# Blocks 4 and 5 of a convolution feeding a gated feed-forward block: from time-major matmuls to channel-major taps

## The chip, the cores and the metric

The kernel runs on one core of one Trainium2 chip. The time is device microseconds (us) of one launch; the kernel before takes 771.22 us, the median of three runs between 770.91 and 771.37 us. Times inside the launch are counted from the start of the profile's span.

The core's engines work through instruction queues of their own, each in the order in which the program gave them: PE (matmuls), ACT, DVE and POOL (element-wise work), and SP, which here only issues transfers. POOL also issues transfers: those that change the type on the way (float32 to float16) are all issued from it.

## The reference

`x` has 8 sequences of 4096 rows (time) with 192 columns (channels). First a causal convolution over time with 7 taps, one softmax-normalised set of taps for each of 8 heads of 24 channels; then a feed-forward block on the 32768 rows:

```python
out[b, s, h, :] = sum(w[h, k] * x_pad[b, s + k, h, :] for k in range(7))
g = y @ w_gate                      # y: (32768, 192), w_gate: (192, 1536)
silu = g * (1.0 / (1.0 + np.exp(-g)))
return (silu * (y @ w_val)) @ w_out # (32768, 192), float32
```

## The kernel before

**Blocks and steps.** The rows are cut into 64 blocks of 512. The inner width of 1536 is cut into 12 chunks of 128, so the work is 768 steps (`n`), 12 for a block; within a block a step is `j`, 0 to 11. Step `n` runs `gate_val` (L734): twelve half-height matmuls of 512 columns in pairs (gate and val side by side) for one chunk, in three pairs over the three channel tiles of the block; ACT then applies Silu (L752) and DVE multiplies by val (L754). At every step with `j` of 1, 4, 7 or 10 a `slot` (L802) runs 24 matmuls of the product with `w_out`; so PE's pattern is three steps and one slot. The slot at `j` of 4 ends a block: ACT and DVE copy the result out of PSUM and SP issues the store.

**The block's input.** `gate_val` needs the convolved block with channels on partitions, as three tiles of float16, `xc[b][0..2]`. They are made in two ways.

- *Time-major, by PE:* blocks 0 to 5. For blocks 2 to 5 `early_pair` (L379) makes two blocks at once: rows are loaded by POOL in windows (tile `xp`), doubled by SP (`twice`), multiplied with a banded matrix of the taps in 64 matmuls of 120 columns (L394), and copied out by ACT and DVE (L411, L422). Blocks 3, 4 and 5 then go to DRAM (`eout`, L424, four transfers each) and come back transposed (`efetch`, L434, three DMA transposes each). `early_pair(2)` stands at step 19, `early_pair(4)` at step 27.
- *Channel-major, by ACT, DVE and POOL:* blocks 6 to 63, in units of four blocks (unit 1 holds blocks 4 to 7, unit 2 blocks 8 to 11). `cast_x` (L542, POOL's queue) copies a unit of `x` to DRAM as float16; `turn_x` (L560, SP's queue) fetches it transposed, two DMA transposes a block; `join_x` (L569) puts the third 64 channels of two blocks side by side. Then three *jobs* for each two blocks (`conv_job`, L580): the first 128 channels of the even block, the shared 64 channels of both ("pair"), and the first 128 channels of the odd block. A job has seven taps: tap 0 on ACT into `total`, taps 1 and 2 on DVE into `total` (L618), taps 3 and 4 on ACT into tiles of their own (L643), which POOL adds (L593), and taps 5 and 6 on POOL, a product (L608) and an addition each. `place` (L653) then copies the shared channels and the joined ones to where `gate_val` reads them: four transfers on SP.

**What sets the order.** The order on each engine is written out by the program (`seq`, L71). `pooled_work` (L708), called once a step, hands out the taps: one DVE tap at `j` of 1, 7 and 10; one ACT tap at those and at 4, two at 10 of even blocks; so one job takes eight steps on average. POOL's part of a job is issued where the last tap before it is issued. A block is placed 14 steps after its last job was issued (`done + 14`), and not before 16 steps ahead of its first step. `planned` (L678) says for each unit at which step the cast, the transposes and the jobs are queued: the first cast at step 11, the next at 12, unit 3's at 56. On SP all transfers stand in one line: stores, transposes, joins and copies; a transfer that has to wait holds up all that stand behind it.

Of the kernel before, what the change touches and what calls it, by code (L numbers as in the profile page):

```python
# [10 lines left out]
def kernel(  # L11
# [422 lines left out]
    def efetch(b):  # L434
        xc[b] = []
        for k in range(SL):
            t = cpool.tile([P, XW], fp16, tag=f"xc{k}", name=f"xc{k}", bufs=8)
            seq(
                nc.sync.dma_start_transpose(
                    out=t[:, 0:TB], in_=scre[b][0:TB, Q * k : Q * k + P]  # L440
                )
            )
            xc[b].append(t)

    def eturn(b, where, then=None):
        c, j = (2, EO) if b < 2 else (4, CO)
        tiles = [
            cpool.tile([P, XW], fp16, tag=f"xc{k}", name=f"xc{k}", bufs=8)
            for k in range(SL)
        ]  # L450
# [28 lines left out]
        xc[b] = tiles  # L479
        if b == 0:  # L480
            copy_channel_taps()
# [41 lines left out]
        for m, name in enumerate(pick):  # L523
            taps[name] = both_taps[:, m * K : m * K + K]

    def first_of(u):
        return HALF if u == 1 else 0

    def head_x(u):
        rows = XP + UT - first_of(u) * TB  # L530
        xs[u] = dpool.tile([rows, D], fp16, tag="xs", name="xs")
        if u % upb == 0:
            seq(
                nc.sync.dma_start(
                    out=xs[u].rearrange("t d -> (t d)")[0 : XP * D].rearrange(
                        "(a n) -> a n", n=P
                    ),
                    in_=fill[0 : XP * D // P, :],
                )
            )  # L540

    def cast_x(u):  # L542
        t0 = u * UT + first_of(u) * TB
        rows = XP + u * UT + UT - t0
        flat = xs[u].rearrange("t d -> (t d)")
        skip = XP if u % upb == 0 else 0
        n = (rows - skip) * D // P
        seq(
            nc.gpsimd.dma_start(  # L549
                out=flat[skip * D : rows * D].rearrange("(a n) -> a n", n=n),  # L550
                in_=bass.AP(
                    tensor=x_flat.tensor,
                    offset=(t0 - XP + skip) * D,
                    ap=[[n, P], [1, n]],
                ),
                max_dma_last_dim=2048,
            )
        )

    def turn_x(u, i, at):  # L560
        r0 = TB * (i - first_of(u))
        rows = xs[u][r0 : r0 + TB + XP]
# [3 lines left out]
        seq(nc.sync.dma_start_transpose(out=t, in_=rows[:, at : at + P]))  # L566
        tiles[u, i] = t
# [1 line left out]
    def join_x(u, i):  # L569
        seq(nc.sync.dma_start(out=x12[u, 2 * i + 1][0:Q], in_=x12[u, 2 * i][Q:P]))  # L570

    FIRST, ON_DVE = 0, (1, 2)
# [7 lines left out]
    def conv_job(u, what, i):  # L580
        index = n_jobs[0]
        n_jobs[0] += 1
        on_act, on_pool = SHARES[index % len(SHARES)]
        job = {"dve": len(ON_DVE), "act": len(on_act), "parts": []}
        at = XP - pad

        def shifted(k):
            return job["src"][:, at + k : at + k + TB]

        def add(part, k):  # L590
            total = job["total"]
            seq(
                nc.gpsimd.tensor_tensor(  # L593
                    job["dst"] if k == K - 1 else total, total, part, op=ALU.add
                )
            )

        def proceed():
            if job["dve"]:
                return  # L600
            while job["parts"]:
                add(*job["parts"].pop(0))
            if job["act"]:
                return
            for k in on_pool:
                part = cpool.tile([P, TB], fp32, tag="piece", name="piece", bufs=2)
                seq(
                    nc.gpsimd.tensor_scalar(  # L608
                        part, shifted(k), scalar1=job["tap"][:, k : k + 1],
                        scalar2=1.0, op0=ALU.mult, op1=ALU.mult,  # L610
                    )
                )
                add(part, k)
            finished[u, what, i] = step_now[0]

        def dve_step(k):
            seq(
# [8 lines left out]
        def act_step(k):  # L626
# [10 lines left out]
                )  # L637
                dve_steps.extend((index, lambda k=k: dve_step(k)) for k in ON_DVE)
            else:
                part = cpool.tile([P, TB], fp32, tag="part", name="part", bufs=8)  # L640
                job["parts"].append((part, k))
# [9 lines left out]
        act_steps.extend((index, lambda k=k: act_step(k)) for k in (FIRST, *on_act))  # L651

    def place(u, i):  # L653
        b = UB * u + i
# [14 lines left out]
    plan = {}  # L669
    placing = []  # L670

    def queue_jobs(u):
        for i in range(first_of(u), UB, 2):
            for job in (("block", i), ("pair", i // 2), ("block", i + 1)):
                conv_job(u, *job)
        placing.extend((u, i) for i in range(first_of(u), UB))

    def planned(v):  # L678
        s0 = ustep * v
        turns = [  # L680
            turn
            for i in range(first_of(v), UB, 2)
            for turn in ((i, 0), (i, Q), (i + 1, Q), (i + 1, 0), (i // 2, None))
        ]
        if v == 1:
            head, cast, jobs = 10, 11, 27
            times = (20, 20, 20, 23, 23)
        elif v == 2:
            head, cast, jobs = 10, 12, 40
            times = (32, 33, 34, 35, 37, 38, 39, 40, 41, 43)  # L690
        elif v == 3:
            head, cast, jobs = 56, 56, 56
            times = range(66, 86, 2)
        else:
            head = cast = s0 - (115 if v > 4 else 100)
            jobs = s0 - 89
            first = s0 - (95 if v > 4 else 87)
            times = range(first, first + 20, 2)
        plan.setdefault(head, []).append(lambda: head_x(v))
        plan.setdefault(cast, []).append(lambda: cast_x(v))  # L700
# [5 lines left out]
        plan.setdefault(jobs, []).append(lambda: queue_jobs(v))  # L706

    def pooled_work(n, j):  # L708
        step_now[0] = n
        if j != 4:  # L710
            ready = dve_steps[0][0] if dve_steps else None
            if j in (1, 7, 10) and ready is not None:
                dve_steps.pop(0)[1]()
            for _ in range(2 if j == 10 and n // NCH % 2 == 0 else 1):
                ahead = act_steps[0][0] if act_steps else n_jobs[0]
                if j in (1, 7, 10) and act_steps and (
                    ready is None or ahead < ready + 3
# [2 lines left out]
        while placing:  # L720
# [133 lines left out]
    for v in range(1, NU):  # L854
        planned(v)

    for n in range(n_steps):
        b, j = divmod(n, NCH)
# [8 lines left out]
        elif j % 3 == 1 and n > 18:  # L867
# [63 lines left out]
```

## Time and profile before

| | before |
|---|---|
| median of 3 runs | 771.22 us |
| profiled execution, its own time | 771.32 us |
| its span in the profile | 769.5 us |
| TensorE clock granted | 1.00 |
| PE busy | 763.0 us, 99% of the span |
| DVE busy | 702.5 us, 91% |
| ACT busy | 649.1 us, 84% |
| POOL busy | 637.8 us, 83% |

The profiled execution's own time is 1.8 us longer than its span; that part lies before the first and after the last recorded instruction. A line of the timeline gives the start in us, the length in us, the engine, the line of the kernel, the operation, what it writes and reads, and how many instructions were merged; in brackets the idle time ahead of it and what ended it. A line of a group gives the busy time, the mean of one instruction in ns, and the idle time just before such instructions with what ended it. The chain that ended last is followed back from the last instruction; its shares say which engine was being waited for.

### The profile page before, as it was taken

The page shows a single profiled execution, that of the slowest core. Times are in us where ns is not written, and L with a number is a line of the kernel's source. Part 1 is how long each engine was busy: PE and PEld are TensorE (multiplying, and loading weights), DVE is VectorE, ACT ScalarE, POOL GpSimd, SP SyncE. Part 2 cuts the span into 40 slices and gives each one's busy share as a digit, 9 for nine tenths or more (in the row PEclk, how much of TensorE's full clock was granted, in tenths as well). Part 3 has the DMA queues.
Part 4 walks back from the last instruction along what each step waited for, and adds up shares of the span by engine and source line. Part 5 has one row for each costly group of instructions (what it writes and reads, how often), then busy time and mean ns, then how long its engine had stood idle before and what let it go on. Part 6 is the DMA issues. An engine that isn't in the chain of part 4 may idle for free.

```text
span 769.5 us, 27729 instructions
## 1 busy us (share of the span) xinstructions
PE 763.0 (99%) x11041; PEld 616.1 (80%) x11041; DVE 702.5 (91%) x1048; ACT 649.1 (84%) x1114; POOL 637.8 (83%) x570
## 2 busy tenths in 40 slices
PE   8999999999999999999999999999999999999997
PEld 5878888888888888888888888888888888888886
DVE  7789999999999999999999999999999999999875
ACT  6688888888888888888888888888888888888764
POOL 8039899999989898998989989999899998889700
PEclk9999999999999999999999999999999999999999
DMA  9966646653536444456443545447454453121211
GB/s 143 198 115 122 154 80 149 128 88 84 123 81 124 106 85 108 99 95 119 92 102 89 100 111 108 92 82 118 92 120 101 82 116 92 53 70 37 71 56 43
DMA packets 145762, 77.52 MB, mean 101 GB/s; under 512 B 79976, under 2 KB 145504, under 8 KB 145632
## 3 DMA queue, kind: packets, MB, share of 16 engines
q1 hardware_dynamic: 126720, 61.05, 34.3%
q0 software_dynamic: 18912, 14.70, 13.8%
q8 instruction: 86, 1.41, 0.8%
q14 instruction: 44, 0.36, 0.2%
HBM read 29.39 MB, written 37.46 MB: 87 GB/s over the span
## 4 chain that ended last, share of the span: by engine, by line
PE 99%; ACT 0%; DVE 0%; issue 0%
PE val L743 51%; PE acc L769 33%; PE gate L743 14%; PE warm L837 0%; PE turn L457 0%; PE acc L790 0%; PE cv L394 0%; PE cv L350 0%; ACT tme L368 0%; DVE h L754 0%; ACT wide L308 0%; ACT o_sb L899 0%; PE taps L295 0%; DVE spread L275 0%; PE ctap L513 0%
## 5 line engine op out<-in xcount | busy, mean ns | idle before, releaser
L754 DVE TENSOR_TENSOR h<-sig,val 128x512 f16<-128x512 f16 x768 | 497.1, 682 | 59.4 <-PE gate L743 54.3
L752 ACT ACTIVATE sig<-gate 128x512 f16<-128x512 f32 x768 | 457.5, 596 | 107.9 <-PE gate L743 78.3
L743 PE MATMUL gate<-pxc,w 64*128 64x512 f16 x2088 | 488.0, 376 | 0.0
L743 PE MATMUL val<-pxc,w 64*128 64x512 f16 x2088 | 488.0, 376 | 0.0
L743 PEld LDWEIGHTS <-w 64*128 64x128 f16 x4608 | 360.1, 110 | 119.7 <-issue 0.7
L769 PE MATMUL acc<-wo,h 64*128 64x192 f16 x6096 | 336.7, 243 | 0.0
L769 PEld LDWEIGHTS <-h 64*128 64x128 f16 x6096 | 311.6, 94 | 21.4 <-ACT sig L752 0.4
L593 POOL TENSOR_TENSOR total<-total,part 128x512 f32<-128x512 f32 x174 | 221.8, 1275 | 73.8 <-DVE total L618 50.0
L618 DVE SCALAR_TENSOR_TENSOR total<-x,both_taps,total 128x512 f32<-128x512 f16 x174 | 186.2, 1070 | 0.0
L608 POOL TENSOR_SCALAR piece<-x,both_taps 128x512 f32<-128x512 f16 x174 | 159.7, 918 | 0.0
L593 POOL TENSOR_TENSOR total<-total,piece 128x512 f32<-128x512 f32 x87 | 123.5, 1419 | 7.3
L643 ACT ACTIVATE part<-x,both_taps 128x512 f32<-128x512 f16 x174 | 124.3, 714 | 0.0
L593 POOL TENSOR_TENSOR pxc<-total,piece 128x512 f16<-128x512 f32 x58 | 74.2, 1279 | 4.8
L643 ACT ACTIVATE total<-x,both_taps 128x512 f32<-128x512 f16 x87 | 62.1, 714 | 0.0
L743 PE MATMUL gate<-xc,w 64*128 64x512 f16 x216 | 51.4, 377 | 0.0
L743 PE MATMUL val<-xc,w 64*128 64x512 f16 x216 | 51.3, 376 | 0.0
L593 POOL TENSOR_TENSOR y<-total,piece 128x512 f16<-128x512 f32 x29 | 36.8, 1271 | 2.4
L821 DVE COPY o_sb<-acc 128x384 f32<-128x384 f32 x63 | 34.5, 548 | 0.0
L820 ACT COPY o_sb<-acc 128x384 f32<-128x384 f32 x63 | 29.6, 471 | 2.6 <-PE acc L769 2.6
L549 POOL DMA_DIRECT2D xs<-in_x_dram x15 | 11.7, 778 | 0.0
L837 PE MATMUL warm<-fill 128*128 128x512 f16 (+1 forms) x12 | 4.1, 500 | 1.0 <-DVE fill L90 1.0
L470 ACT COPY xc<-turn 128x520 f16<-128x520 f16 (+1 forms) x5 | 2.9, 588 | 1.0 <-PE turn L457 0.9
(66 smaller groups left out, 55.8 us busy)
## 6 DMA issues: line engine op xcount, KB each, us to landing
out_dram<-o_sb SPq DMA_DIRECT2D x63, 384.0 KB
pxc<-pxc SPq DMA_DIRECT2D x116, 64.0 KB
pxc<-y SPq DMA_DIRECT2D x116, 64.0 KB
xs<-in_x_dram POOLq DMA_DIRECT2D x7, 774.0 KB, 8.6
xs<-in_x_dram POOLq DMA_DIRECT2D x7, 768.0 KB, 7.0
x<-x SPq DMA_DIRECT2D x29, 66.0 KB
x<-xs SPq DMA_TRANSPOSE x116
xp<-in_x_dram POOLq DMA_DIRECT2D x4, 240.0 KB, 7.5
```

What stands on the lines that cost most here:

```text
L549: nc.gpsimd.dma_start(out=flat[skip * D : rows * D].rearrange("(a n) -> a n", n=n), in_=bass.AP(tensor=x_flat.tensor, offset=(t0 - XP + sk ...
L593: nc.gpsimd.tensor_tensor(job["dst"] if k == K - 1 else total, total, part, op=ALU.add)
L608: nc.gpsimd.tensor_scalar(part, shifted(k), scalar1=job["tap"][:, k : k + 1], scalar2=1.0, op0=ALU.mult, op1=ALU.mult,)
L618: nc.vector.scalar_tensor_tensor(job["total"], shifted(k), job["tap"][:, k : k + 1], job["total"], op0=ALU.mult, op1=ALU.add,)
L643: nc.scalar.activation(part, shifted(k), AF.Copy, scale=job["tap"][:, k : k + 1])
L743: nc.tensor.matmul(o, w16[m][p0 : p0 + Q, k, e::E], xc[b][k][p0 : p0 + Q, 0:TB], start=(k == 0), stop=(k == SL - 1),)
L752: silu[n] = seq(nc.scalar.activation(sg, g, AF.Silu)).ins
L754: seq(nc.vector.tensor_tensor(hj, sg, v, op=ALU.mult))
L769: nc.tensor.matmul(acc[b][bank][:, s, :], hj[p0 : p0 + Q, ts(2 * bank + s, P)], wo16[p0 : p0 + Q, j, :], start=(not second and j == 0 and ...
L820: seq(nc.scalar.copy(o_sb[:, 0:2, :], acc[b][0]))
L821: seq(nc.vector.tensor_copy(o_sb[:, 2:4, :], acc[b][1]))
L837: nc.tensor.matmul(warm[:, 0:width], fill, fill.unsqueeze(1).to_broadcast([P, width // P, P]), start=True, stop=True, skip_group_check=True,)
```

## The change

Blocks 4 and 5 take the channel-major way as well. `early_pair(4)`, its two row loads and doublings, the `eout` of blocks 4 and 5 and their `efetch` go. Unit 1 gets three more jobs (90 in all instead of 87). Its cast is split in two halves of two blocks each: the first at step 11 as before, the second at step 23. The steps at which casts, transposes and jobs of units 1 to 3 are queued move; the join now stands before the last of each group of four transposes instead of behind it. The first two jobs get one more DVE tap (at `j` of 4) and one more ACT tap (at 7 and at 10). Within a job, POOL now sums its own product of tap 5, ACT's taps 3 and 4, and tap 6 into a tile `rest` as they come, and adds `rest` to `total` at the end; it was one chain on `total` that began after DVE's taps. A job has the same six POOL instructions as before. `place` comes 5 steps after the last job was issued (2 for block 4) instead of 14. Some tiles get fewer buffers (`xc` 4 instead of 8, `part` 4 instead of 8).

```diff
-    for e in (2, 4):
-        xp[e] = cpool.tile([P, 4 * EG, D], fp16, tag="xp", name="xp")
-        for r in range(2):
-            windows(xp[e], Q * r, (e + r) * TB, CO, 0, 4 * EG)
-        twice(xp[e])
+    xp[2] = cpool.tile([P, 4 * EG, D], fp16, tag="xp", name="xp", bufs=1)
+    for r in range(2):
+        windows(xp[2], Q * r, (2 + r) * TB, CO, 0, 4 * EG)
+    twice(xp[2])
...
+    def part_of(u, i):
+        return (u, i // HALF * HALF, HALF) if u == 1 else (u, 0, UB)
...
-    SHARES = ((3, 4), (5, 6)), ((3, 4), (5, 6)), ((3, 4), (5, 6))
+    FIRST, ON_DVE, ON_ACT, ON_POOL = 0, (1, 2), (3, 4), (5, 6)
+    soon = 2
...
         def proceed():
-            if job["dve"]:
-                return
-            while job["parts"]:
-                add(*job["parts"].pop(0))
-            if job["act"]:
-                return
-            for k in on_pool:
...
-                add(part, k)
-            finished[u, what, i] = step_now[0]
+            if job["dve"] == 0 and job["act"] == 0:
+                add(job["dst"], job["total"], job["rest"])
+                finished[u, what, i] = step_now[0]
...
-            if k != FIRST:
-                job["act"] -= 1
-                proceed()
+            if k == FIRST:
+                job["rest"] = product(ON_POOL[0])
+                return
+            add(job["rest"], job["rest"], part)
+            job["act"] -= 1
+            if job["act"] == 0:
+                for k in ON_POOL[1:]:
+                    add(job["rest"], job["rest"], product(k))
+            proceed()
...
-            for turn in ((i, 0), (i, Q), (i + 1, Q), (i + 1, 0), (i // 2, None))
+            for turn in ((i, 0), (i, Q), (i + 1, Q), (i // 2, None), (i + 1, 0))
         ]
-        if v == 1:
-            head, cast, jobs = 10, 11, 27
-            times = (20, 20, 20, 23, 23)
+        if v == 1 and i0 == 0:
+            head, cast, jobs = 10, 11, 21
+            times = (16, 16, 16, 18, 19)
+        elif v == 1:
+            head, cast, jobs = 10, 23, 35
+            times = (30, 30, 31, 33, 34)
         elif v == 2:
-            head, cast, jobs = 10, 12, 40
-            times = (32, 33, 34, 35, 37, 38, 39, 40, 41, 43)
+            head, cast, jobs = 10, 38, 55
+            times = range(47, 57)
         elif v == 3:
-            head, cast, jobs = 56, 56, 56
-            times = range(66, 86, 2)
+            head, cast, jobs = 62, 62, 82
+            times = range(72, 92, 2)
...
+        ready = dve_steps[0][0] if dve_steps else None
+        if ready is not None and (j in (1, 7, 10) or (j == 4 and ready < soon)):
+            dve_steps.pop(0)[1]()
         if j != 4:
-            ready = dve_steps[0][0] if dve_steps else None
-            if j in (1, 7, 10) and ready is not None:
-                dve_steps.pop(0)[1]()
-            for _ in range(2 if j == 10 and n // NCH % 2 == 0 else 1):
+            many = (j == 10 and n // NCH % 2 == 0) or (
+                act_steps and act_steps[0][0] < soon and j != 1
+            )
+            for _ in range(2 if many else 1):
...
-            if n < max(done + 14, ustep * u + NCH * i - 16):
+            if n < max(done + (2 if (u, i) == (1, 0) else 5), ustep * u + NCH * i - 16):
...
-        if n in (19, 27):
-            early_pair(2 if n == 19 else 4)
+        if n == 19:
+            early_pair(2)
...
-        elif n in (28, 29):
-            eout(n - 24)
-        elif n in (30, 36):
-            efetch(4 if n == 30 else 5)
```

`place` itself is unchanged: the order on SP after the change is, for the blocks that the prediction speaks of, as the steps above give it: the second half-unit's transposes (steps 30 to 34), the copies of block 4 (step 36), the first transpose of unit 2 (47), the copies of block 5 (48), the other transposes and joins of unit 2 (48 to 56), the copies of block 6 (63).

More of the change, by code (lines that the diff above doesn't have):

```diff
@@ L436, in efetch @@
         for k in range(SL):
-            t = cpool.tile([P, XW], fp16, tag=f"xc{k}", name=f"xc{k}", bufs=8)
+            t = cpool.tile([P, XW], fp16, tag=f"xc{k}", name=f"xc{k}", bufs=4)
             seq(
@@ L447, in eturn @@
         tiles = [
-            cpool.tile([P, XW], fp16, tag=f"xc{k}", name=f"xc{k}", bufs=8)
+            cpool.tile([P, XW], fp16, tag=f"xc{k}", name=f"xc{k}", bufs=4)
             for k in range(SL)
@@ L524, in copy_channel_taps, with head_x @@
             taps[name] = both_taps[:, m * K : m * K + K]
[L526 to L531, printed above, removed]
+    def part_of(u, i):
+        return (u, i // HALF * HALF, HALF) if u == 1 else (u, 0, UB)
+    def head_x(part):
+        u, i0, n = part
+        xs[part] = dpool.tile([XP + n * TB, D], fp16, tag=f"xs{n}", name="xs")
         if u % upb == 0:
@@ L534, in head_x @@
                 nc.sync.dma_start(
-                    out=xs[u].rearrange("t d -> (t d)")[0 : XP * D].rearrange(
+                    out=xs[part].rearrange("t d -> (t d)")[0 : XP * D].rearrange(
                         "(a n) -> a n", n=P
@@ L540, in head_x, with cast_x @@
             )
[L542 to L545, printed above, removed]
+    def cast_x(part):
+        u, i0, n = part
+        t0 = u * UT + i0 * TB
+        rows = XP + n * TB
+        flat = xs[part].rearrange("t d -> (t d)")
         skip = XP if u % upb == 0 else 0
@@ L560, in turn_x @@
     def turn_x(u, i, at):
-        r0 = TB * (i - first_of(u))
-        rows = xs[u][r0 : r0 + TB + XP]
+        part = part_of(u, i)
+        r0 = TB * (i - part[1])
+        rows = xs[part][r0 : r0 + TB + XP]
         tiles = (x01, x12)[at // Q]
@@ L570, in join_x @@
         seq(nc.sync.dma_start(out=x12[u, 2 * i + 1][0:Q], in_=x12[u, 2 * i][Q:P]))
-    FIRST, ON_DVE = 0, (1, 2)
-    SHARES = ((3, 4), (5, 6)), ((3, 4), (5, 6)), ((3, 4), (5, 6))
+    FIRST, ON_DVE, ON_ACT, ON_POOL = 0, (1, 2), (3, 4), (5, 6)
+    soon = 2
     act_steps = []
@@ L582, in conv_job @@
         n_jobs[0] += 1
-        on_act, on_pool = SHARES[index % len(SHARES)]
-        job = {"dve": len(ON_DVE), "act": len(on_act), "parts": []}
+        job = {"dve": len(ON_DVE), "act": len(ON_ACT)}
         at = XP - pad
@@ L588, in shifted, with add, product @@
             return job["src"][:, at + k : at + k + TB]
-        def add(part, k):
-            total = job["total"]
-            seq(
-                nc.gpsimd.tensor_tensor(
-                    job["dst"] if k == K - 1 else total, total, part, op=ALU.add
+        def add(to, one, two):
+            seq(nc.gpsimd.tensor_tensor(to, one, two, op=ALU.add))
+        def product(k):
+            tag = "rest" if k == ON_POOL[0] else "piece"
+            part = cpool.tile([P, TB], fp32, tag=tag, name=tag, bufs=2)
+            seq(
+                nc.gpsimd.tensor_scalar(
+                    part, shifted(k), scalar1=job["tap"][:, k : k + 1],
+                    scalar2=1.0, op0=ALU.mult, op1=ALU.mult,
                 )
             )
+            return part
         def proceed():
-            if job["dve"]:
-                return
-            while job["parts"]:
-                add(*job["parts"].pop(0))
-            if job["act"]:
-                return
-            for k in on_pool:
[L606 to L612, printed above, removed]
-                add(part, k)
-            finished[u, what, i] = step_now[0]
+            if job["dve"] == 0 and job["act"] == 0:
+                add(job["dst"], job["total"], job["rest"])
+                finished[u, what, i] = step_now[0]
         def dve_step(k):
@@ L639, in act_step @@
             else:
-                part = cpool.tile([P, TB], fp32, tag="part", name="part", bufs=8)
-                job["parts"].append((part, k))
+                part = cpool.tile([P, TB], fp32, tag="part", name="part", bufs=4)
             seq(
@@ L646, in act_step @@
             )
-            if k != FIRST:
-                job["act"] -= 1
-                proceed()
-        act_steps.extend((index, lambda k=k: act_step(k)) for k in (FIRST, *on_act))
+            if k == FIRST:
[7 more added lines that the diff above has]
+            proceed()
+        act_steps.extend((index, lambda k=k: act_step(k)) for k in (FIRST, *ON_ACT))
     def place(u, i):
@@ L670, with queue_jobs, planned @@
     placing = []
-    def queue_jobs(u):
-        for i in range(first_of(u), UB, 2):
+    def queue_jobs(part):
+        u, i0, n = part
+        for i in range(i0, i0 + n, 2):
             for job in (("block", i), ("pair", i // 2), ("block", i + 1)):
                 conv_job(u, *job)
-        placing.extend((u, i) for i in range(first_of(u), UB))
-    def planned(v):
+        placing.extend((u, i) for i in range(i0, i0 + n))
+    def planned(part):
+        v, i0, n = part
         s0 = ustep * v
@@ L681, in planned @@
             turn
-            for i in range(first_of(v), UB, 2)
-            for turn in ((i, 0), (i, Q), (i + 1, Q), (i + 1, 0), (i // 2, None))
-        ]
-        if v == 1:
-            head, cast, jobs = 10, 11, 27
-            times = (20, 20, 20, 23, 23)
+            for i in range(i0, i0 + n, 2)
+            for turn in ((i, 0), (i, Q), (i + 1, Q), (i // 2, None), (i + 1, 0))
+        ]
+        if v == 1 and i0 == 0:
[4 more added lines that the diff above has]
+            times = (30, 30, 31, 33, 34)
         elif v == 2:
-            head, cast, jobs = 10, 12, 40
-            times = (32, 33, 34, 35, 37, 38, 39, 40, 41, 43)
+            head, cast, jobs = 10, 38, 55
+            times = range(47, 57)
         elif v == 3:
-            head, cast, jobs = 56, 56, 56
-            times = range(66, 86, 2)
+            head, cast, jobs = 62, 62, 82
+            times = range(72, 92, 2)
         else:
@@ L698, in planned @@
             times = range(first, first + 20, 2)
-        plan.setdefault(head, []).append(lambda: head_x(v))
-        plan.setdefault(cast, []).append(lambda: cast_x(v))
+        plan.setdefault(head, []).append(lambda: head_x(part))
+        plan.setdefault(cast, []).append(lambda: cast_x(part))
         for m, turn in enumerate(turns):
@@ L705, in planned @@
             plan.setdefault(times[m], []).append(todo)
-        plan.setdefault(jobs, []).append(lambda: queue_jobs(v))
+        plan.setdefault(jobs, []).append(lambda: queue_jobs(part))
     def pooled_work(n, j):
         step_now[0] = n
+        ready = dve_steps[0][0] if dve_steps else None
+        if ready is not None and (j in (1, 7, 10) or (j == 4 and ready < soon)):
+            dve_steps.pop(0)[1]()
         if j != 4:
-            ready = dve_steps[0][0] if dve_steps else None
-            if j in (1, 7, 10) and ready is not None:
-                dve_steps.pop(0)[1]()
-            for _ in range(2 if j == 10 and n // NCH % 2 == 0 else 1):
+            many = (j == 10 and n // NCH % 2 == 0) or (
+                act_steps and act_steps[0][0] < soon and j != 1
+            )
+            for _ in range(2 if many else 1):
                 ahead = act_steps[0][0] if act_steps else n_jobs[0]
@@ L853 @@
     make_band()
-    for v in range(1, NU):
-        planned(v)
+    planned(part_of(1, 0))
+    planned(part_of(1, HALF))
+    for v in range(2, NU):
+        planned(part_of(v, 0))
     for n in range(n_steps):
```

## Prediction

> **What bounds the kernel now.** I read the page's busy shares and its chain first. PE is busy for 99% of the span and the chain is PE; so a change pays only by work taken from PE, and costs where PE has to wait.
>
> ```profile
> span 769.5 us, 27729 instructions
> PE 763.0 (99%) x11041; PEld 616.1 (80%) x11041; DVE 702.5 (91%) x1048; ACT 649.1 (84%) x1114; POOL 637.8 (83%) x570
> ...
> PE 99%; ACT 0%; DVE 0%; issue 0%
> ```
>
> Then PE's timeline around `early_pair(4)`. Slots start every 2.93 us (40.12, 43.05, and so on to the end without a gap); here the distance is 4.32.
>
> ```profile
> 35.80 1.19 PE L769 MATMUL acc<-wo,h 64*128 64x192 f16 x23
> ...
> 38.30 0.46 PE L394 MATMUL cv<-xp,band 64*32 64x120 f16 x33
> 39.00 0.40 PE L394 MATMUL cv<-xp,band 64*32 64x120 f16 x31 [0.24 <-DVE h L754]
> ...
> 40.12 1.16 PE L769 MATMUL acc<-wo,h 64*128 64x192 f16 x22
> ...
> 43.05 1.16 PE L769 MATMUL acc<-wo,h 64*128 64x192 f16 x22
> ```
>
> Third, PE's first matmul on a block made by taps (block 6, step 72), then SP's and POOL's timelines before it. The block's last copy is issued at 75.33 and by its completion count lands at 82.08: 0.7 us ahead of PE.
>
> ```profile
> 82.81 0.38 PE L743 MATMUL gate<-pxc,w 64*128 64x512 f16 x1
> ```
>
> ```profile
> 71.25 0.47 SPq L570 DMA_DIRECT2D x<-x  x1
> 71.83 1.28 SPq L824 DMA_DIRECT2D out_dram<-o_sb  x1
> 73.21 0.47 SPq L667 DMA_DIRECT2D pxc<-pxc  x1
> 73.77 1.51 SPq L667 DMA_DIRECT2D pxc<-y  x2
> 75.33 0.59 SPq L667 DMA_DIRECT2D pxc<-pxc  x1
> 77.36 0.38 SPq L824 DMA_DIRECT2D out_dram<-o_sb  x1
> 81.22 1.93 SPq L566 DMA_TRANSPOSE x<-xs  x1
> ```
>
> ```profile
> 70.57 1.27 POOL L593 TENSOR_TENSOR pxc<-total,piece 128x512 f16<-128x512 f32 x1
> 71.78 0.84 POOL L549 DMA_DIRECT2D xs<-in_x_dram  x1
> ```
>
> The cast issued at 71.78 lands at 81.20, when SP's waiting transpose starts. The completion counts say more: the join at 71.25 landed after 2.7 us, but the store at 71.83 after 9.5, the four copies after 8.3 to 6.8, the store at 77.36 after 5.4: all 0.2 to 1.6 us behind the cast. The cast at 111.60 held the store and copies of 112.5 to 114.9 in the same way. Copies with no cast under way land after 2.0. So a cast holds what SP issues behind it.
>
> **The change part by part.** *PE.* `early_pair(4)` goes: 4.32 − 2.93 = 1.39 us (its matmuls alone are 0.86; the rest is the idle time and the refill around them). This is all that can be won: from there on no other distance between slots is longer than 2.93. It moves step 72's first matmul to 82.81 − 1.39 = 81.42, its third channel tile 0.43 later, to 81.85.
>
> *ACT, DVE.* Three jobs add nine ACT taps of 0.71 and six DVE taps of 0.75 (POOL idle) to 1.12 (POOL busy); the ACT and DVE copies of L411 and L422 go. Between 35 and 43 us both are idle for about a fifth of the time, which hides it. One place shows: step 22 has two ACT taps before the Silu of step 23, and the slot of step 25 waits for that Silu. The Silu of step 22 ended at 34.11; two taps (1.36 as they overlap) and a Silu of 0.60 make 36.1, against a slot at 35.80. I take 0.2, bounds 0 and 0.4. Later double taps follow a Silu that is earlier and fit.
>
> *Blocks 4 and 5.* The first half's cast is issued behind two row loads and `band`, about 16.4; the second of two loads landed at 21.2, and the first cast of before (the same size) 4.5 us behind its last load, so about 25.7. Its transposes (1.29 each in the queue, 2.7 to landing) are there at 28 to 34, before ACT needs them at 34. The second half's cast stands behind POOL's first addition, issued about 37 and landed at 43 (5 to 7 us for half a cast of 6.7 to 9.4). Its four transposes and join, the join now waiting 1.4 for the third transpose to land, leave SP free at 50; POOL's last addition for block 4 ends at 49.5. Four copies of 0.62 and 2.0 of landing: 54, needed at step 48, 57.97. Four us of slack, but a cast issued before 52 would take it.
>
> *POOL, and unit 2's cast.* This cast was at 18.34 with nothing ahead; now it stands at step 38 behind all of jobs A (block 4) and B (pair) and most of C (block 5). From A's fourth tap (ACT, step 25, done about 37.5) POOL has no gap: rest of A, add, product, add, 3.6; B's product 0.9; A's last addition 1.3; B 6.2; C up to its tap 6, 5.8 (additions 1.28 to 1.42, products 0.92, by their groups). Sum 17.8: issued at 55.3. Even units' casts took 6.7 to 8.0; SP is idle, so 7.0: landed at 62.3.
>
> *SP's line.* The first transpose of unit 2 (step 47) waits for that, and behind it in the line stand the copies of block 5 (step 48) and, after all eight transposes, those of block 6. Block 5: 62.3 + 1.3 + 4 × 0.62 + 1.4 = 67.5, needed at step 60, about 69.7: in time. Block 6: up to the seventh transpose 1.3 + 2.5 (copies) + 2.6 + 1.4 + 0.6 (join) + 1.3 + 0.5 (store) + 2.6 = 12.8, so 75.1; SP's timeline also shows one issue in 8 to 9 us that takes about 1 us more (1.28 and 1.93 above), two of them here: 77.1. It lands 2.7 later, 79.8; join 0.6, last transpose 1.3, last copy 1.9 later and 2.0 to land: 85.6. Without the two long issues 83.6. Needed at 81.85. Here the stall that was 0.7 us away in the trace is real: 1.8 to 3.8 us by SP's line alone.
>
> *Unit 3's cast on top.* It stands at step 62 behind POOL's work for F (block 7). E's second DVE tap (step 58: slot at 68.06, tap 1.42 later as at 59.14, 1.12 long) ends at 70.6; POOL then has E's last addition, F's product, two additions, product, addition: 7.1. Issued at 77.7, landed 8.2 to 9.4 later (odd units), 8.8: 86.5. The copies of block 6 are issued at 82 to 84 and land 0.3 to 0.9 behind it: 87.4. Stall 87.4 − 81.85 = 5.5.
>
> The Trainium skill, DMA: Bandwidth & Descriptors, Queues, rings and completion order, says that each DMA engine takes turns between the queues, a packet at a time; by that the copies would pass the cast, the stall be 3.8 and the sum 773.9. The rows of 71.83 to 77.36 say otherwise, and I go by them.
>
> *Behind it.* Copies of block 7 land about 90 and of block 8 about 105, against 98 and 110 with the stall; from unit 5 on a block is copied 9 to 12 steps ahead of its use and a cast is issued right after, so no further stall. POOL has the same six instructions per job and the last jobs end 18 steps later, with their copies 12 steps ahead: nothing.
>
> **Sum.** The profiled execution took 771.32 (span 769.5 and 1.8 around it), 0.1 over the median, which is nothing here. 771.3 − 1.4 + 0.2 + 5.5 = 775.6.
>
> **The rivals.** *Block 6 is in time (not slower).* The place is the copies of block 6, the price the 5.5. It needs the last copy by 81.85, so unit 2's cast to land before 60.5 even without long issues on SP, 1.8 earlier than summed, and no hold by unit 3's cast. For it: POOL's products take 0.69 as often as 1.13, worth 1 us. Against: 17.8 us of POOL work without a gap, and each transfer ahead. Time 770.1, within 0.2%.
>
> *The seventh transpose is caught too.* It starts about 77.1, unit 3's cast at 77.7. If its data is held until 86.5, the join behind it waits as well, and join, transpose and copies follow: 86.8 + 0.6 + 1.3 + 1.9 + 2.0 = 92.6, or 93 with a long issue: stall 11, 781.0. For it: 0.6 us between them, and a store issued 0.05 after a cast was caught. Against: the join 0.53 ahead of a cast was not. One more long issue, or unit 2's cast 0.5 later, decides.
>
> *The cast holds nothing here* (the copies pass, or unit 3's cast is late): SP's line alone, 1.8 to 3.8: 771.9 to 773.9.
>
> *The change doesn't do what it says:* block 4's or 5's copies late at step 48 or 60. It takes a delay of 4 or 2 us, and moves step 72 by as much, so it replaces part of the stall rather than adding to it; it lies within the cases.
>
> **How the numbers follow.** The forecast 0.43 (own range 774 to 777.5, from the cast's 8.2 to 9.4 and the 0.2); caught 0.26 (779.5 to 782.5); nothing held 0.17; in time 0.14. About 0.2%, 1.5 us, is what a measurement can tell from no change. Slower: 0.43 + 0.26 + most of 0.17 = 0.82. Same: 0.14 and a little = 0.15, as 1.39 us is under the bound; faster 0.03. Range 771.7 to 782.3: it leaves out 0.14 below and some 0.04 above.
>
> **What would show it.** Right: no L394 after 30 us; slots 2.93 apart up to step 70; a gap on PE at its first or third matmul pair of step 72, near 81.5, ended by a copy of L667, of 4 to 6 us; unit 2's cast near 55 and unit 3's near 78; SP waiting for unit 2's cast some 8 us. Wrong: step 72 starts with no gap, or the copies land 2 us after issue although the cast is under way, or the casts are issued 3 us earlier.

## The result and the profile after

The kernel after the change takes 779.61 us (median of 4 runs, 778.54 to 780.40), the kernel before 771.30 on the same chip (770.91 to 771.51): a ratio of 1.0107, with a 95% interval of 1.0090 to 1.0125. It is slower by 8.3 us, where 4.4 had been forecast. The profiled execution took 780.25 us, with a span of 778.5, 9.0 us longer than that of before.

The page after: span and busy shares (part 1), the granted TensorE clock by slices of 19.5 us (part 2), and the shares of the chain that ended last (part 4).

```profile
span 778.5 us, 27617 instructions
...
PE 766.7 (98%) x10977; PEld 733.7 (94%) x10977; DVE 708.6 (91%) x1050; ACT 653.2 (84%) x1121; POOL 647.9 (83%) x587
...
PEclk9999899999999999999999999999999999999999
...
PE 97%; DMA 1%; DVE 1%; ACT 0%; issue 0%; POOL 0%; DVEq 0%
```

PE lost 64 matmuls, as the change says, and yet is busy for 3.7 us longer; the chain now holds a share of DMA; and one slice of the clock, 78 to 97 us, reads 8 instead of 9. Where the time went is seen best from the start of the first gate matmul of a step in both traces:

| step | before, us | after, us | difference |
|---|---|---|---|
| 0 | 8.84 | 9.61 | +0.77 |
| 20 | 30.11 | 30.81 | +0.70 |
| 28 | 39.33 | 38.86 | −0.47 |
| 32 | 44.04 | 44.02 | −0.01 |
| 50 | 61.63 | 62.47 | +0.83 |
| 73 | 83.45 | 90.17 | +6.71 |
| 76 | 86.39 | 95.64 | +9.25 |
| 767 (last) | 762.50 | 771.75 | +9.25 |

The first row is the launch itself: over the kernels run below it lies between −0.02 and +0.77 whatever was changed. Another 0.30 is lost at steps 7 to 9 and 0.37 won at step 20. At step 28 the pair is gone (with step 29 the difference goes from +0.78 to −0.60), at 32 and 50 something is lost, at 72 to 76 most of it; from there on nothing moves for over 670 us.

The slots of steps 22, 25 and 28 in PE's timeline after, where the trace of before had a distance of 4.32:

```profile
33.56 1.20 PE L775 MATMUL acc<-wo,h 64*128 64x192 f16 x23
...
36.57 1.21 PE L775 MATMUL acc<-wo,h 64*128 64x192 f16 x24
...
39.51 1.20 PE L775 MATMUL acc<-wo,h 64*128 64x192 f16 x24
```

They stand 3.01 and 2.94 apart: the second pair of blocks is gone from PE, and the two ACT taps of step 22 cost the slot of step 25 some 0.07.

PE's timeline after, around step 72 (83.64 is its first channel tile):

```profile
83.64 0.38 PE L749 MATMUL gate<-pxc,w 64*128 64x512 f16 x1
...
89.28 0.58 PE L749 MATMUL gate<-pxc,w 64*128 64x512 f16 x1 [5.26 <-DMA pxc<-pxc]
89.57 0.58 PE L749 MATMUL val<-pxc,w 64*128 64x512 f16 x1
89.79 0.58 PE L749 MATMUL gate<-pxc,w 64*128 64x512 f16 x1
90.00 0.58 PE L749 MATMUL val<-pxc,w 64*128 64x512 f16 x1
...
91.45 2.18 PE L775 MATMUL acc<-wo,h 64*128 64x192 f16 x23
...
96.29 1.18 PE L775 MATMUL acc<-wo,h 64*128 64x192 f16 x23
```

PE has done the first channel tile of step 72 and waits 5.26 us for the second, half of which the first of block 6's four copies brings. By their completion counts the copies land at 89.24, 89.53, 89.74 and 89.96, and the four matmuls from 89.28 on each start 0.04 to 0.05 us behind one of them: gate and val of the second tile, then of the third. So step 73 starts 5.88 us late (6.71 − 0.83); that is what the copies cost, and it is the stall that was predicted. What was not predicted stands behind it: the slot at 91.45 takes 2.18 us, where the next takes 1.18. The same in a window (length, then busy time and count of PE, PEld, DVE, ACT and POOL, granted clock, DMA share, GB/s):

```profile
89.00:95.00 6.00, 5.72 (x42) 4.44 (x43) 2.04 (x3) 1.92 (x4) 1.19 (x1) 0.50 0.65 158
```

After the idle time the granted clock is 0.50; in its records from 88.51 to 95.34, 6.83 us. Between step 73 and 76 another 2.54 us are lost (9.25 − 6.71) with no wait to be seen.

Why the copy was late is read from SP's timeline after:

```profile
54.23 0.40 SPq L830 DMA_DIRECT2D out_dram<-o_sb  x1
63.82 1.13 SPq L567 DMA_TRANSPOSE x<-xs  x1
...
74.71 5.18 SPq L567 DMA_TRANSPOSE x<-xs  x3
81.39 0.47 SPq L571 DMA_DIRECT2D x<-x  x1
81.90 1.43 SPq L567 DMA_TRANSPOSE x<-xs  x1
83.43 0.57 SPq L665 DMA_DIRECT2D pxc<-pxc  x1
84.09 1.19 SPq L665 DMA_DIRECT2D pxc<-y  x2
85.34 0.69 SPq L665 DMA_DIRECT2D pxc<-pxc  x1
```

and from the casts in POOL's timeline after:

```profile
57.12 0.76 POOL L549 DMA_DIRECT2D xs<-in_x_dram  x1
...
80.30 0.82 POOL L549 DMA_DIRECT2D xs<-in_x_dram  x1
```

SP stands idle from 54.6 to 63.8 for unit 2's cast (issued 57.12, landed 63.80), then works its line off; the copies of block 6 come at 83.43 to 85.34, when unit 3's cast (issued 80.30, landed 88.37) is under way. They land 5.8 to 4.6 us after issue, where a copy takes 2.0 without a cast.

The two smaller losses are waits of a slot for DVE, each 0.5 to 0.9 us on PE's path. DVE's timeline after, at both places:

```profile
41.78 0.55 DVE L827 COPY o_sb<-acc 128x384 f32<-128x384 f32 x1
42.24 0.95 DVE L611 SCALAR_TENSOR_TENSOR total<-x,both_taps,total 128x512 f32<-128x512 f16 x1
...
59.45 2.19 DVE L611 SCALAR_TENSOR_TENSOR total<-x,both_taps,total 128x512 f32<-128x512 f16 x1
```

and PE's slots that waited:

```profile
43.85 0.34 PE L775 MATMUL acc<-wo,h 64*128 64x192 f16 x4 [0.21 <-DVE h L760]
...
62.29 0.34 PE L775 MATMUL acc<-wo,h 64*128 64x192 f16 x4 [0.58 <-DVE h L760]
```

At step 28 DVE has the output copy and, right behind it, the extra tap of `j` 4, so its products for the slot of step 31 are late. At 59.45 a tap of 0.75 to 1.1 us takes 2.19; beside it POOL runs two additions from 59.83 to 62.77.

### The profile page after: what moved, and what is told of

It is laid out like the page before. It is cut to its first block, busy times and chain, and to the rows that moved or that the text cites. A ratio compares the mean times of both kernels' runs of the same rounds, so it can differ in the third digit from the quotient of the medians.

```text
span 778.5 us, 27617 instructions
## 1 busy us (share of the span) xinstructions
PE 766.7 (98%) x10977; PEld 733.7 (94%) x10977; DVE 708.6 (91%) x1050; ACT 653.2 (84%) x1121; POOL 647.9 (83%) x587
## 4 chain that ended last, share of the span: by engine, by line
PE 97%; DMA 1%; DVE 1%; ACT 0%; issue 0%; POOL 0%; DVEq 0%
PE val L749 33%; PE gate L749 32%; PE acc L775 30%; DMA pxc<-pxc 1%; PE warm L843 1%; DVE h L760 0%; PE turn L456 0%; PE acc L796 0%; POOL pxc L591 0%; PE cv L349 0%; ACT tme L367 0%; PE cv L393 0%; ACT wide L307 0%; DVE total L611 0%; ACT sig L758 0%
## 5 line engine op out<-in xcount | busy, mean ns | idle before, releaser
L749 PE MATMUL gate<-pxc,w 64*128 64x512 f16 x2160 | 507.1, 377 | 5.3 <-DMA pxc<-pxc 5.3
L749 PE MATMUL val<-pxc,w 64*128 64x512 f16 x2160 | 506.9, 377 | 0.0
L749 PEld LDWEIGHTS <-w 64*128 64x128 f16 x4608 | 448.9, 110 | 21.7 <-issue 6.2
L591 POOL TENSOR_TENSOR rest<-rest,part 128x512 f32<-128x512 f32 x180 | 259.4, 1441 | 29.2 <-ACT part L635 19.5
L591 POOL TENSOR_TENSOR rest<-rest,piece 128x512 f32<-128x512 f32 x90 | 126.9, 1410 | 7.5
L591 POOL TENSOR_TENSOR pxc<-total,rest 128x512 f16<-128x512 f32 x60 | 76.3, 1272 | 29.2 <-PE val L749 19.6
L597 POOL TENSOR_SCALAR rest<-x,both_taps 128x512 f32<-128x512 f16 x90 | 63.5, 705 | 10.5 <-DMA x<-xs 10.4
L597 POOL TENSOR_SCALAR piece<-x,both_taps 128x512 f32<-128x512 f16 x90 | 62.5, 694 | 0.0
L591 POOL TENSOR_TENSOR y<-total,rest 128x512 f16<-128x512 f32 x30 | 38.2, 1272 | 20.2 <-DVE total L611 19.5
L749 PE MATMUL gate<-xc,w 64*128 64x512 f16 x144 | 34.3, 378 | 0.0
```

Source lines behind the costliest of these rows:

```text
L591: seq(nc.gpsimd.tensor_tensor(to, one, two, op=ALU.add))
L597: nc.gpsimd.tensor_scalar(part, shifted(k), scalar1=job["tap"][:, k : k + 1], scalar2=1.0, op0=ALU.mult, op1=ALU.mult,)
L749: nc.tensor.matmul(o, w16[m][p0 : p0 + Q, k, e::E], xc[b][k][p0 : p0 + Q, 0:TB], start=(k == 0), stop=(k == SL - 1),)
```

## The experiments

Every time below is compared with the kernel before, run on the same chip (medians 771.49 to 771.66).

**The clock alone** (`e1_keep_clock`). The stall stays; PE gets 24 of the filler matmuls that the kernel's start already has, written to a bank that is overwritten next.

```diff
+        if n == 6 * NCH:
+            warm = ppool.tile([P, TB], fp32, tag="gate", name="warm")
+            keep_warm(24)
```

> Changed kernel with 24 dummy matmuls of 128x512 on PE ahead of step 72 (24 x 0.213 = 5.1 us, inside the wait of 5.4). Clock theory: PE waits as long for block 6's copies (first matmul on the copied tile at 89 to 90 us), but the half clock that the changed kernel's rows show from 89 to 95 us (0.50) does not come, and the 3.0 us that it costs go: some 776.6 against 779.6. Rival (the slow steps behind the wait are the refilling of PSUM banks and the queues of ACT and DVE): the steps 72 to 76 stay as slow and the time stays at 779 to 780.

777.11 us (777.02 to 777.46), ratio 1.0071 [1.0056, 1.0086]. PE's timeline of this kernel:

```profile
83.31 5.35 PE L843 MATMUL warm<-fill 128*128 128x512 f16 x24
...
89.24 0.37 PE L749 MATMUL gate<-pxc,w 64*128 64x512 f16 x1 [0.23 <-DMA pxc<-pxc]
```

The second channel tile starts at 89.24 as before (89.28 after the change), but its matmul takes 0.37 instead of 0.58, no half clock is recorded until the work ends, and the loss is complete by step 73: 6.0 us there, against 5.9 after the change, and nothing behind it. So the clock cost 2.5 us of the 8.3 by the medians (2.8 by the two ratios), as much as the trace shows between steps 73 and 76, and the copies cost the rest. The 3.0 that had been expected counted 0.5 to the clock that the four copies cost by landing one after the other. The Trainium skill, TensorE: Matmul & The Clock Gate, Part 1: The HAM clock gate, states this rule: the array runs at half clock after an idle window of about 3.4 us, and such windows are free-running. The windows of 3.41 us and the 0.50 seen here agree with it; that a window must be idle throughout does not hold for the next kernel, as the last section shows.

**Unit 3's cast later** (`e2_unit3_late`): does the cast hold the copies, or is it SP's line alone?

```diff
-            head, cast, jobs = 62, 62, 82
+            head, cast, jobs = 62, 68, 82
```

> Changed kernel with unit 3's cast queued at step 68 instead of 62, all else as it is. Theory of two causes (SP's line and the hold by unit 3's cast): with no cast under way the copies of block 6, issued at 83.4 to 85.3, land 2.0 later, the last at 86 to 87.4 instead of 90.0; PE's wait at step 72 shrinks from 5.4 to 1.5 to 3.5 us, and 2 to 4 us go, 5 if the shorter wait leaves the clock alone: 774.5 to 777.5. Rival (SP's line alone, the cast holds nothing): copies and wait as in the changed kernel, 779.6. Rival (block 6's taps are late): no change either.

777.84 us (777.49 to 778.34), 1.0079 [1.0063, 1.0096]. SP's timeline of this kernel:

```profile
82.02 0.54 SPq L665 DMA_DIRECT2D pxc<-pxc  x1
82.65 1.25 SPq L665 DMA_DIRECT2D pxc<-y  x2
83.95 0.59 SPq L665 DMA_DIRECT2D pxc<-pxc  x1
```

its POOL's:

```profile
83.69 0.82 POOL L549 DMA_DIRECT2D xs<-in_x_dram  x1
```

and its PE's:

```profile
84.25 0.37 PE L749 MATMUL gate<-pxc,w 64*128 64x512 f16 x1 [0.70 <-DMA pxc<-pxc]
...
85.40 0.37 PE L749 MATMUL gate<-pxc,w 64*128 64x512 f16 x1 [0.27 <-DMA pxc<-y]
88.20 0.58 PE L749 MATMUL val<-pxc,w 64*128 64x512 f16 x1 [2.43 <-DMA pxc<-pxc]
```

This tells the two apart inside one kernel. The three copies issued before the cast land 2.1 to 2.2 us after issue. The fourth, 0.26 us behind the cast, takes 4.2. The store and the copies of block 7, issued at 84.63 to 87.14, take 9.5 to 7.7 and land at 94.1 to 94.8, just behind the cast at 93.37. The cast holds what is issued behind it. The gain of 1.8 us is a little under the 2 to 4 that were expected, because one copy was still caught and the clock halved all the same.

**Unit 2's cast early** (`e3_unit2_early`): undo the wait of SP's line for this cast, which starts the whole chain.

```diff
-            head, cast, jobs = 10, 38, 55
+            head, cast, jobs = 10, 12, 55
```

> Changed kernel with unit 2's cast back at step 12, as before the change; all else as it is. Theory: SP no longer waits 9.6 us for that cast at step 47, its line runs ahead, block 6's copies are placed before 72 us, and the wait at step 72 (5.4) and the half clock behind it (3.0) both go: 771.2, between 770.4 and 772. Rival (taps of block 6 late on POOL or DVE): a wait at step 72 stays, above 774.

771.68 us (770.65 to 774.09, 10 runs), 1.0006 [0.9997, 1.0016]. No wait at step 72 and no half clock: 7.9 of the 8.3 us are back with one number changed. Left are the losses at steps 32 (0.56) and 50 (0.53) and a new one at step 97 (0.97): block 8's copies now stand behind unit 3's transposes, whose cast took from 78.99 to 89.66.

**POOL's new order alone** (`e4_rest_only`): the kernel before, with only the sum of POOL's share in `rest` taken over.

```diff
-            while job["parts"]:
-                add(*job["parts"].pop(0))
...
+            if k == FIRST:
+                job["rest"] = product(ON_POOL[0])
+                return
+            add(job["rest"], job["rest"], part)
```

> Kernel before with only POOL's order inside a job changed: its own product, ACT's two taps and its second product summed into rest, joined to total last; blocks 4 and 5 stay time-major and a block is still placed 14 steps after. If the new order costs PE something in itself (POOL's additions beside DVE's taps make these longer): 772.5 or more. If it is neutral: 771.3 within 0.5, with DVE's taps at their 1.07 us mean.

771.49 us (771.17 to 772.35), 0.9999 [0.9990, 1.0009]: nothing, although the additions of ACT's taps have a mean of 1440 ns in it against 1275 before.

**The join last again** (`e5_join_last`): the order of transposes and join as before the change.

```diff
-            for turn in ((i, 0), (i, Q), (i + 1, Q), (i // 2, None), (i + 1, 0))
+            for turn in ((i, 0), (i, Q), (i + 1, Q), (i + 1, 0), (i // 2, None))
```

> Changed kernel with the join again behind the last of its four transposes. SP then waits less for the third transpose to land: its line to block 6 is up to 2 x 1.3 us shorter, the copies are issued at 81 to 83 instead of 83.4 to 85.3. Theory (unit 3's cast, issued at 80.3 and landed at 88.4, holds them): they land at 88.5 to 89.5 all the same, the wait at step 72 loses at most 1 us, and the time is 778.5 to 779.6. Rival (SP's line sets the wait): the wait falls by 2 to 2.6 us, 777 or less.

777.83 us (777.44 to 778.23), 1.0083 [1.0070, 1.0097]. SP's timeline of this kernel (the first and the last copy of block 6):

```profile
81.12 0.55 SPq L665 DMA_DIRECT2D pxc<-pxc  x1
...
83.09 0.67 SPq L665 DMA_DIRECT2D pxc<-pxc  x1
```

its POOL's:

```profile
79.54 0.82 POOL L549 DMA_DIRECT2D xs<-in_x_dram  x1
```

and its PE's:

```profile
87.85 0.58 PE L749 MATMUL gate<-pxc,w 64*128 64x512 f16 x1 [4.59 <-DMA pxc<-pxc]
```

The copies are issued 2.3 us earlier, 0.8 of it because this launch began earlier (PE's wait begins at 83.3, not 84.0), so 1.5 earlier against PE. But they land at 87.81 to 88.82, still 6.7 to 5.7 us after issue; the wait is 0.67 shorter, and step 73 starts 5.38 us late instead of 5.88. So most of the stall is the cast's, under way from 79.54 to 88.65, and not SP's line. The time fell by 1.8, outside what was expected and more than the stall did. In the profiled execution the half clock lasted 3.41 us (87.5 to 90.9) instead of 6.83, and 1.0 us is lost behind step 73 instead of 2.54: that makes the rest. The mean clocks of the other runs (0.995 to 0.997) show that it varies from run to run.

**Both casts early** (`e6_both_early`): e3, and unit 3's cast at step 24.

```diff
-            head, cast, jobs = 62, 62, 82
+            head, cast, jobs = 24, 24, 82
```

> Changed kernel with unit 2's cast at step 12 and unit 3's at step 24, behind the second half of unit 1's. With unit 2's cast alone moved (771.68) the trace has no wait at step 72 but one of 1.0 us at step 96, where block 8's copies stand behind unit 3's transposes and its cast, which landed at 89.7. Theory: that wait goes too; 770.7, between 770.2 and 771.3. What is left over the ideal are the slots of steps 31 and 49 (0.56 and 0.53), where DVE is late. Rival (the copies of block 8 are late for POOL or DVE): the wait at step 96 stays, 771.7. If unit 3's cast, landing near 47, holds the copies of block 4 instead, a wait at step 48.

772.39 us (771.32 to 772.96, 11 runs), 1.0011 [1.0002, 1.0020]: a miss. The loss at step 97 is gone, but the cast, issued at 37.50 and landed at 48.63, held something else. PE's timeline:

```profile
48.50 0.37 PE L749 MATMUL gate<-xc,w 64*128 64x512 f16 x1 [0.37 <-DMA xc<-scre]
```

Two transposes of block 3 (`efetch`), issued at 37.59 and 38.89, landed at 48.46 and 48.90; the step that needs them starts 0.83 us late. Step 30 loses 0.69 too, where a matmul waits for a product of DVE; why that one is late was not looked for.

**Without the extra DVE taps** (`e7_no_extra_dve`): e6, without the tap at `j` of 4 (and 2 steps of delay for every `place`).

```diff
-        if ready is not None and (j in (1, 7, 10) or (j == 4 and ready < soon)):
+        if ready is not None and j in (1, 7, 10):
...
-            if n < max(done + (2 if (u, i) == (1, 0) else 5), ustep * u + NCH * i - 16):
+            if n < max(done + 2, ustep * u + NCH * i - 16):
```

> As the kernel with both casts early, without the extra DVE tap at j of 4 for the first two jobs, and every block placed 2 steps after its last job. Theory: the 0.56 us at the slot of step 31 come from that tap (it stands behind the o_sb copy and ahead of the products that the slot waits for), so they go: 770.1 to 770.4. All later jobs end a DVE tap, three steps, later; if that makes a block late, a wait at step 48, 72 or 96 appears and the time is 771 or more.

773.59 us (772.14 to 774.70, 7 runs), 1.0028 [1.0017, 1.0038]: a miss too. The loss at step 32 is gone with the extra taps (that at step 50 is absent from e6 already). But POOL's last addition for block 6 starts only at 77.92, and step 72 loses 1.76. The profiled launch also lost 1.19 by step 20, which the other kernels don't; for the longest wait in that stretch, 1.4 us in `early_pair`, the profile names no releaser.

**Half the filler** (`e8_half_warm`): e1 with 12 matmuls, to see how short an idle stretch costs the clock.

```diff
-            keep_warm(24)
+            keep_warm(12)
```

> Changed kernel with 12 dummy matmuls ahead of step 72 instead of 24: 2.6 of the 5.4 us of wait are filled, 2.8 idle. If the granted clock falls only after a longer idle time than that, it stays at 1.00 and the time is that of the 24, 777.1. If it falls after less (the kernel with unit 3's cast late had waits of 0.7, 0.3 and 2.4 us in a row and a clock of 0.50 behind them), the half clock is back: 779 to 780.

779.15 us (777.36, 779.15, 779.16, 779.83), 1.0103 [1.0088, 1.0119]. The idle stretch in the profiled run is 2.82 us; that run kept the clock (mean 1.000) and is the fastest, the three others have 0.997 and are 1.8 to 2.5 us longer. So one kernel does both. A window of 3.41 us at half clock can take 1.7 at most (half of it); what the slower runs lose beyond that is not explained.

**The casts apart from what they hold** (`e9_casts_apart`). If a cast holds what SP issues during its 7 to 11 us, it belongs where SP issues nothing urgent: unit 2's behind POOL's first product (28.85 to 38.39), unit 3's at step 44 (60.21 to 68.69), and the join last.

```diff
+                if index == 0:
+                    for todo in plan.pop("first", ()):
+                        todo()
...
-            for turn in ((i, 0), (i, Q), (i + 1, Q), (i // 2, None), (i + 1, 0))
+            for turn in ((i, 0), (i, Q), (i + 1, Q), (i + 1, 0), (i // 2, None))
...
-            head, cast, jobs = 10, 38, 55
+            head, cast, jobs = 10, "first", 55
...
-            head, cast, jobs = 62, 62, 82
+            head, cast, jobs = 44, 44, 82
```

> Changed kernel with the casts kept clear of the copies: unit 2's issued by POOL right after its first product (about 29 us, landed near 37), unit 3's at step 44 (about 59, landed near 67), the join behind its four transposes. Theory: no wait at steps 36, 48, 60, 72 and 96; what stays are the two late products of DVE at the slots of steps 31 and 49 (0.55 and 0.5 to 0.85); 771.5 - 1.4 - 0.4 + 1.2 = 770.9, between 770.4 and 771.4. If a cast still holds a block's copies, a wait ended by a copy is in the trace and the time is above 771.5.

771.01 us (770.21 to 771.91, 11 runs) against 771.66 before (21 runs): 0.9991 [0.9982, 0.9999]. No wait for a copy is left; the losses at steps 32 (0.55) and 50 (0.53) are.

**The first extra tap elsewhere** (`e10_tap_at_23`): e9, with the extra DVE tap at step 23 instead of at `j` of 4, so that it doesn't stand behind an output copy.

```diff
-        if ready is not None and (j in (1, 7, 10) or (j == 4 and ready < soon)):
+        if ready is not None and (j in (1, 7, 10) or n == 2 * NCH - 1):
```

> As the kernel with the casts apart, with the one extra DVE tap at step 23, where DVE has no other tap, instead of step 28, where it stands behind the o_sb copy. Theory: the slot of step 31 no longer waits for the product of step 29, 0.5 us less: 770.4, and the tap of all later jobs at the same steps. Rival (the slot is late for the two ACT taps at step 22 or for POOL beside DVE): the 0.55 stay, 770.9.

770.65 us (770.40 to 771.03, 11 runs), 0.9987 [0.9978, 0.9996]: faster than both kernels, than the one before by 0.13%, between 0.04 and 0.22. SP's timeline of this kernel, the copies of block 6:

```profile
77.90 0.55 SPq L668 DMA_DIRECT2D pxc<-pxc  x1
78.54 1.19 SPq L668 DMA_DIRECT2D pxc<-y  x2
79.78 0.59 SPq L668 DMA_DIRECT2D pxc<-pxc  x1
```

and PE's waits, all that its trace gives:

```profile
PE warm L846 <- DVE fill L90: 1.0, 1, 1.0
PE cv L349 <- ACT wide L307: 0.6, 1, 0.6
PE turn L456 <- ACT tme L367: 0.5, 1, 0.5
PE acc L778 <- DVE h L763: 0.3, 1, 0.3
```

The copies are issued 5.5 us earlier than after the change and land after 2.0, in time. The loss at step 32 is gone, which shows its cause: the tap right behind the output copy. A quarter of a us is lost at step 28 instead (1.00 is won there, 1.25 in the other changed kernels), and 0.70 at step 50 remain; neither was looked into by itself.

## Why the prediction was right or wrong

**Right.** *PE.* The pair's end was worth 1.38 at steps 28 and 29 against 1.39; `early_pair(2)` gave 0.37 more (an idle 0.20 inside it is gone), which had not been foreseen. *The stall.* The step (72), the releaser (copies of block 6) and the mechanism (unit 2's late cast puts SP's line late, unit 3's cast then holds the copies) came out; e3, e2 and e5 each confirm one link. The size is near: with the third tile due 0.43 behind the first, at 84.07, and the last copy landed at 89.96, it is 5.9 against 5.5. In a detail it differs: PE stopped at the second tile, for the first copy, where "its first or third matmul pair" was named. *The summed chain.* Unit 2's cast was issued at 57.1 and landed at 63.8 (55.3 and 62.3 predicted), SP waited 9.2 us for it (some 8), unit 3's cast came at 80.3 (77.7). POOL's stretch before unit 2's cast took 18.9 instead of 17.8: it did have a gap, 0.69 for a DVE tap, and additions of up to 1.7. The copies, issued at 83.4 to 85.3 (82 to 84 predicted), still fell behind that cast. Blocks 4 and 5 were in time, their copies landed by 55.2 and 70.1. *The rivals.* The seventh transpose was issued at 77.35 (77.1 predicted) and landed at 81.37, not caught, as the cast came 3 us behind it instead of 0.6; block 6 was not in time; and the cast did hold.

**Wrong: the sum has no term for the clock.** The step is "771.3 − 1.4 + 0.2 + 5.5 = 775.6". It counted a stall of 5.5 as 5.5. An idle PE of that length also loses its clock: 2.5 us in the profiled execution and 2.5 by e1 against the medians. The same term is missing from the rivals with a stall. The trace of before had no idle stretch of that length ahead of its end, so nothing in it called for the term; e1 and e8 now give it.

**Wrong: the cover for DVE.** The step "Between 35 and 43 us both are idle for about a fifth of the time, which hides it" took an average over 8 us. In the traces, DVE was busy for all of 40 to 44 and of 56 to 64 us after the change, and the products that a slot waits for stood behind the tap: 0.56 at step 32 and 0.85 at step 50. The one place that was priced, the slot of step 25, took 0.07 instead of 0.2; "slots 2.93 apart up to step 70" did not hold. "Later double taps follow a Silu that is earlier and fit" looked at ACT; the extra DVE tap behind the output copy was never placed on DVE's own line.

**Against the time.** From 775.6 to the profiled 780.25: the clock 2.5, the stall 0.4 more, DVE and ACT 1.5 where 0.2 stood, a launch that began 0.8 later and lost 0.3 more by step 9, less 0.4 for the pairs (1.38 + 0.37 against 1.39) and 0.3 for an end that is shorter. That makes 4.6 of the 4.65, as near as these can be read. The direction, the place and the stated range held; the forecast case's own range, 774 to 777.5, did not. The measured 779.61 falls into the range of a rival that did not come (the seventh transpose caught, 779.5 to 782.5), and only because the stated range was stretched over that rival does it hold the result. That is luck: the mechanism was right, the number was not. Had the clock and the two DVE places been priced, the sum would have been near 779.

**The rule that was weighed.** The row was right against the turn-taking between queues that the prediction cited: the copies behind a cast did not pass. The same section of the Trainium skill (DMA: Bandwidth & Descriptors, Queues, rings and completion order) also states that a completion count is written only after every earlier write of that DMA engine, across its queues. By that alone the copies could look late although their data is there. The packets in the trace tell the two apart. DMA packets of the kernel after (q0 carries the cast, q1 what SP issues; packets, MB, share of the 16 engines), first from 81.5 to 84.5 us, then from 84.5 to 87:

```profile
q0 software_dynamic: 516, 0.40, 101.5%
...
q0 software_dynamic: 440, 0.34, 97.2%
q1 hardware_dynamic: 188, 0.09, 19.0%
```

SP issues the join at 81.39, and until 84.5 not one packet of its queue moves; the join of before, issued at 71.25 ahead of a cast, began at 72.38. Then packets of both queues run side by side, as turn-taking has it. The four copies are 256 packets of 1024 bytes, and the first of these starts at 87.11; before the change the copies issued at 73.21 to 75.33 start at 79.60. So the data itself is late, and not only its count. Why SP's queue stands still at first, no run here tells. Nor is the cast's end a fixed bound: in e1 the join, issued 0.6 us behind the cast, landed 2.4 us before it.

## What to carry to other kernels

A transfer that sits on one queue can be late because of one on another: before a large cast is moved, list what the other queue issues in the 7 to 11 us behind its issue, and put the cast where that list holds nothing urgent. When a change leaves an otherwise dense PE idle for some 3 us or more, price the stall plus 1 to 2.5 us for the clock (1.0 for one half-clock window in e5, 2.5 for two after the change), and remember that filler matmuls save the second part only. Slack of an engine is read at the instruction that someone waits for, in order, and not from its idle share over several us.

## What the runs showed of the hardware

**The clock looks at windows, not at gaps.** In the traces' records the granted clock changes at distances of a multiple of 3.41 us (6.83 is two of them, 81.92 is 24). Windows cut at these boundaries show what each did. First the kernel after (columns as in the windows above; the clock is that of the window itself):

```profile
81.69:85.10 3.41, 2.33 (x38) 1.54 (x33) 3.41 (x4) 2.27 (x4) 3.33 (x4) 1.00 1.10 148
85.10:88.51 3.41, 0.00 (x0) 0.00 (x0) 0.73 (x2) 0.00 (x0) 3.19 (x3) 1.00 1.21 191
88.51:91.93 3.42, 2.65 (x16) 1.79 (x17) 0.69 (x1) 0.84 (x2) 0.00 (x0) 0.50 0.92 254
91.93:95.34 3.41, 3.41 (x33) 2.85 (x30) 1.35 (x2) 1.42 (x3) 1.53 (x2) 0.50 0.39 55
```

Then the window of e2 before its clock fell:

```profile
82.81:86.22 3.41, 1.85 (x11) 0.59 (x8) 2.08 (x3) 1.14 (x3) 3.39 (x4) 1.00 0.55 93
```

and one of e8, which kept its clock:

```profile
84.30:87.71 3.41, 2.02 (x10) 0.73 (x9) 1.02 (x2) 0.00 (x0) 3.33 (x3) 1.00 1.23 165
```

A window with PE busy for 2.33 or 2.02 of 3.41 us kept the full clock for the next; one with 1.85 (e2), its idle time in several pieces, lost it; one with 2.65 at half clock (after) did not win it back. So a window need not be wholly idle to cost the clock: in e2 no idle piece before the fall was longer than 0.70 us (PE's ends are modelled, so the busy times are rough). Here the measurement goes beyond the rule of the skill that is cited at e1. Where a stall falls against the windows then decides between no, one (e5) and two windows at half clock (after): in e8 the one run at a clock of 1.000 took 1.8 us less than the next. The exact bound was not looked for.

**A long tap on DVE lies beside long additions on POOL.** A DVE tap has 737 ns at the least and 2.19 us at the most after the change, and the 2.19 lies beside two POOL additions that took 2.94 instead of 2.5. That the one causes the other was read from the trace and not tried.
